# Attention with normalised queries and keys: one score tile moved, shared places for the third shift, a ring of 50, a one-product query scaling

## The chip, the cores and the metric

One core of a Trainium2 chip runs the whole kernel in one launch. The metric is the device time of an execution in microseconds; lower is better. The profile times one execution: its span runs from the first to the last instruction.

The engines are called PE (TensorE, with PEld for its weight loads), DVE (VectorE), ACT (ScalarE), POOL (GpSimd) and SP (SyncE, which here only issues DMAs). Each runs its own queue in order; semaphores tie them together.

## The reference

32 heads, 2048 positions, head size 20, everything in bfloat16. Queries and keys are brought to length one, the scores are scaled by one number per head, and softmax attention follows:

```
qn = q / (sqrt((q * q).sum(-1)) + eps)
kn = k / (sqrt((k * k).sum(-1)) + eps)
logits = einsum('bhqd,bhkd->bhqk', qn, kn) * t[None, :, None, None]
out = einsum('bhqk,bhkd->bhqd', softmax(logits), v)
```

So there are 32 x 2048 x 2048 scores, each of which needs an exponential, a product over 20 elements before it and one over 2048 positions behind it.

## The kernel before

**Units, waves, groups.** The scores of a head are cut into 64 units of 128 keys by 512 queries; four units (one for each group of 512 queries) make a tile, 16 tiles a head. Tiles go two ways. `DVE_TILES` (line 780) says how many of a head's tiles go to DVE: 5 to 7, 203 in all. The other 1236 units go to ACT.

**ACT's way.** Units are taken in waves of 2 and 3 in turn (`WAVES`), each with a slot of its own in `psA`. PE makes the scores (L1148 with 32 rows, or L1155 with 64 rows through the zero-padded `qz`), ACT takes the exponential of a whole wave in one instruction (L1254) and writes it to `p_ring`, a ring of `NP = 40` units. PE multiplies four units with `vaug`, V with a column of ones, into `psF` (L1176). An exponential may overwrite a place of the ring once the product that read it is done: `war` in `add_wave` (L1251) names that product.

**DVE's way.** A tile's scores come from `qP` (L1160), a scaled copy of the queries, as two matrix products into `psF`. The queries and keys carry three extra columns, which add the constants. DVE reads the 1024 sums per partition once (L1305), with one multiply and one add, as 32-bit integers into `xt`: each word holds two 16-bit floats, a bf16 and an fp16, which are approximate exponentials of two scores, so the 2048 scores of a partition's two query groups lie in 1024 words. Three more versions, each shifted by a constant of `PHASES`, are made by integer additions into `ss[0]`, `ss[1]` and `ss[2]`; the four versions are multiplied with V, scaled by `vph` (L959) for each shift, and so averaged (L1176, four sets of four matrix products of 512 columns).

A shift can be made in several ways: on POOL as an addition of 64-bit integers (L1335), in pieces or joined with the same shift of the next tile; on DVE as one addition (L1325), for two tiles at once (L1330), or, for the third shift alone, in a gapped form (L1323) that writes rows of 16 words at a pitch of 17 into a buffer of its own, `sp`. `xt` has `NX = 7` places, `ss[j]` and `sp` have `NE = 4`. `last_use` lists who last used a place; the third shift's list covers the plain and the gapped form together, so both buffers advance together.

**Preparation of a head.** Loads of q, k, v (L838); squares, sums and a reciprocal square root on DVE (L996 to L1024); the normalised rows to `qkn` (L1042); a transposing DMA to `qkT`; DMAs that copy keys in rotated order to `kR` and queries to `qz`. `qP` is made by DVE from `qkT` (L1052) as `qkT * pcol[:, 0] + pcol[:, 1]`, a scale and an addend per partition. Head 0 goes a faster way at the start: PE transposes, POOL copies the keys in three rotated orders (`rotk0`, L1128), and SP transposes these with three DMAs (L1130) to `kR`. The fills of constants stand ahead of that on DVE and POOL (L872 to L909); `kx` and the f32 queries of head 0 lie for that time in the last six units of `p_ring`.

**What sets the order.** A planner in the program (`Program.list_schedule`) simulates the engines with durations written at each `add` and fixes each queue's order before launch. Each task has a priority, mostly its due time in heads. Twenty-seven settings steer its choices, such as how long PE waits for a coming score product, or how many products of the last head may be left when the output bank is handed on (`FLIP`, `FSOON`). `STAGES` gives one number for each 10 us of planned time, which picks a value for each setting. `plan_waits` then writes the semaphore waits. Operations of DVE that the planner calls heavy, all but the reads, transposes and gapped shifts, are kept apart from POOL's additions.

The end of each head: DVE transposes the output (L1192), divides by the sums (L1201, L1209), SP stores.

Of the kernel before, what the change touches and what calls it, by code (L numbers as in the profile page):

```python
# [10 lines left out]
BF16 = mybir.dt.bfloat16  # L11
# [35 lines left out]
PAD = 16  # L47
# [34 lines left out]
class Program:  # L82
# [26 lines left out]
        "EASE": (0.0, 0.15, 0.3), "TWO": (1, 0), "HTR": (0.15, 0.0, 0.3, 0.5), "CONT": (1, 0), "HB": (1.2, 0.5, 0.8, 1.8, 2.4), "HLATE": (1.5, 0.5, 3.0),  # L109
        "WAITH": (0.3, 0.1, 0.6), "BLOG": (5, 3, 4, 7, 9, 99), "PTWO": (1, 0), "STAY": (1, 0), "URGE": (3, 2, 4, 6), "BOOST": (1.0, 0.0, 0.4, 4.0), "DPV": (0.0, 0.3, 0.65, 1.0), "FLIP": (0, 2, 4), "FSOON": (0.3, 0.0, 0.8), "JOIN": (0.8, 0.0, 0.4, 1.4), "MERGE": (0.0, 0.2, 0.4)}  # L110
    STAGES = (5971968, 5971971, 23941566379011, 52142628583944, 59302454818874, 69347322273448, 69347310327784, 70172875370728, 70172839538920, 69760057110760, 69699858183784, 80456615377947, 81282177248715, 81288065602227, 60796380404643, 60796380404648, 60803367607208, 60803367607208, 60829167996776, 68259239759720, 36985831402607, 71631643783891, 71633220411085, 71633220245185, 70033688337794, 70033690079630, 83314320437263, 27171772496628, 49440268483813, 34580101090789, 34580101090789, 34605895514005, 34605919401877, 34599469427608, 15611119408984, 15611107465048, 16436672321368, 16230281107289, 16230281107289, 37177604416007, 37177604416007, 6311176060947, 6311176060947, 13741312038101, 28601477959013, 75896859232048, 75896847288256, 68466969587152, 68466969587152, 75877676995213, 75829302561268, 75880900364788, 73400623713478, 73400086236358, 73400086237510, 83123322387687, 83123322387687, 83123322387687, 83123322387687, 82710539959527)

# [633 lines left out]
def bass_standalone__qk_norm__prompt_kernel(  # L746
# [12 lines left out]
    GORD = (0, 2, 1, 3)  # L759
    NP = 40  # L760
    NB = 8
    NV = 6
    NN = 4
    NT = 3
    NX = 7
    NE = 4
# [12 lines left out]
    DLM = 2  # L779
    DVE_TILES = [5, 6, 6, 6, 7, 6, 7, 6, 7, 6, 7, 6, 7, 6, 7, 6, 6, 7, 6, 7, 6, 7, 6, 7, 6, 7, 6, 7, 6, 7, 6, 5]  # L780
    NDMAX = 8
# [8 lines left out]
    with ExitStack() as es:  # L790
# [11 lines left out]
        vph = sbuf("vph", [128, NV, len(PHASES), NDMAX, 32], FP16)  # L802
        pcol = sbuf("pcol", [128, 2], F32)
        sqs = sbuf("sq", [128, NSQ * 2 * R, D], BF16)
# [87 lines left out]
        zc = [add("POOL", "z", lambda e, tk: e.memset(pcol[:, 0:1], 1.0), 0.06, [], -98.9)]  # L892
        for g, val in ((3, HI_SCALE), (2, 1.0), (1, HI_SCALE)):
            zc.append(add("POOL", "z", lambda e, tk, g=g, val=val: e.affine_select(
                pcol[:, 0:1], pcol[:, 0:1], [[1, 1]], ALU.is_ge, val, base=-32 * g, channel_multiplier=1),
                0.12, [zc[-1]], -98.8 + 0.01 * (3 - g)))
        zc.append(add("POOL", "z", lambda e, tk: e.memset(pcol[:, 1:2], 0.0), 0.06, [zc[-1]], -98.6))
        for p0, val in [(32 * g + D + i, x) for g in range(NG) for i, x in enumerate(
                (LO_REST,) if g % 2 else (HI_REST + HI_SHIFT * HI_SCALE, ROUND, -ROUND))]:
            zc.append(add("POOL", "z", lambda e, tk, p0=p0, val=val: e.affine_select(  # L900
                pcol[:, 1:2], pcol[:, 1:2], [[1, 1]], ALU.not_equal, val, base=-p0, channel_multiplier=1),
                0.12, [zc[-1]], -98.5 + 0.001 * p0))
        z_qz = [memset("POOL", qz[i][:, :, :], 0.0, 0.8, -81.5 + 0.1 * i) for i in range(NZ)]
        z_xt = [memset("POOL", xt[0][:, :].rearrange("p (n w) -> p n w", w=TILE)[:, :, 2048:TILE], 0.0, 0.2, -82)]
# [146 lines left out]
        def add_qp(h, deps):  # L1051
            qp[h] = add("DVE", f"qp{h}", lambda e, tk: e.tensor_scalar(  # L1052
                qP[h % NT][:, :], qkT[h % NT][:, 0:512], pcol[:, 0:1], pcol[:, 1:2], ALU.mult, ALU.add),
                0.323, deps + zc[-1:] + ([lambda: qk_users[h - NT]] if h >= NT else []), h - QLEAD if h else -26.1)
# [32 lines left out]
        def first_head(rinv):  # L1087
# [38 lines left out]
            for dl in range(1, 4):  # L1126
                for (g0, s0, m) in ((0, dl, 4 - dl), (4 - dl, 0, dl)):
                    cp.append(add("POOL", "rotk0", lambda e, tk, dl=dl, g0=g0, s0=s0, m=m: e.tensor_copy(  # L1128
                        kv[:, dl, :, g0:g0 + m, :], kv[:, 0, :, s0:s0 + m, :]), 0.2 + 0.11 * m, [nk], -90 + dl))
            rot[0] = [add("SP", "trnr0", lambda e, tk, dl=dl: e.dma_start_transpose(  # L1130
                kR[0][:, dl - 1, :].rearrange("p (c n) -> p c n", n=128), kx[:, 512 * dl:512 * dl + 512]), 1.3,
# [150 lines left out]
        def add_dgroup(jg):  # L1282
            j, = D_groups[jg]
            h, c, dl = D_tiles[j]
            ox, oe = place(0, NX, 1), place(1, NE, 1)
            bx, be = TILE * ox, TILE * oe
            old = lambda n, o: last_use.get((n, o), [])
# [4 lines left out]
            for bs in ((0,), (1,)) if SPLIT[j % len(SPLIT)] else ((0, 1),):  # L1292
# [17 lines left out]
                if TWICE[j % len(TWICE)]:  # L1310
                    reads.append(read(f"t1b.{j}.{bs[0]}", ss[2][0], be, W_ADD + PHASE_W[2], [qk] + old("s2", oe), due - 4.99))
                    again.append(reads[1])
# [3 lines left out]
            for i in range(len(PHASES)):  # L1316
                dst = ss[i][0]
                if i == 2 and again:
                    sh.append(again)
                    continue  # L1320
                def f_s(e, tk, i=i, dst=dst):
# [6 lines left out]
                def f_two(e, tk, i=i, dst=dst):  # L1328
                    a, b = (x[:, o:o + 2 * TILE].bitcast(I32).rearrange("p (n w) -> p n w", n=2)[:, :, 0:1024] for x, o in ((dst, be), (xt[0], bx)))
                    return e.tensor_scalar(a, b, float(PHASE_W[i]), None, ALU.add)  # L1330
# [3 lines left out]
                if jg >= 2:  # L1334
                    f.alt = lambda c, n, i=i, dst=dst: lambda e, tk: e.int64_add(  # L1335
                        dst[:, be + 2 * c:be + 2 * (c + n)].bitcast(I64), xt[0][:, bx + 2 * c:bx + 2 * (c + n)].bitcast(I64),
                        PHASE_W[i] * 0x100000001)
# [6 lines left out]
            def half(tile, o, g, f):  # L1344
                if f and f[0].slow:
                    return sp[:, oe, 512 // PAD * (g // 2):512 // PAD * (g // 2 + 1), :].bitcast(
                        FP16 if g % 2 else BF16).rearrange("p r (n w) -> p r n w", w=2)[:, :, 0:PAD, 1 - g % 2]
# [6 lines left out]
            for i, (tile, o, dep) in enumerate([(xt[0], bx, t1s)] + [(ss[n][0], be, sh[n]) for n in range(len(PHASES))]):  # L1354
                src = [] if i == 0 else dep
# [83 lines left out]
```

## Time and profile before

| | us |
|---|---|
| median of three runs | 579.21 (579.07 to 581.45) |
| the profiled execution | 579.11 |
| its span | 577.4 |
| ACT: busy / exponentials L1254, union of 495 | 563.0 / 559.5 |
| ACT: first exponential starts, last one ends | 8.03, 570.11 |
| DVE: busy; reads L1305, 203 x 1.217 | 556.7; 247.0 |
| DVE: gapped third shifts L1323, 159 x 1.222 | 194.0 |
| POOL: busy; additions L1335, 403 x 1.116 | 454.3; 442.4 |
| PE: busy | 551.6 |
| granted clock of PE | 1.0 |

In a row of the profile's groups stand the line, engine and operation, then what is written and read with shapes, the count, the busy time in us and the mean length of one in ns, and behind the second bar the idle time of the engine just before and what ended it. In the timeline a row can hold several instructions of one kind (x4): start, length of the whole row, engine, line. Where instructions of one engine overlap, busy time is their union, and the mean length is more than the distance between two of them.

### The profile page before, as it was taken

The numbers are of one execution on the slowest core, as the hardware profiler recorded it, in microseconds if no ns is written. First come the engines' busy times: TensorE is split into PE (matmuls) and PEld (weight loads), VectorE is DVE, ScalarE is ACT, GpSimd is POOL, SyncE is SP. The second block draws the span as 40 slices with busy tenths as digits, with TensorE's granted clock in tenths as the row PEclk, the third lists the DMA queues.
The fourth block names the chain that finished last, engine by engine and source line by source line (L and its number), as shares of the span: only waits on it lengthen the run. The fifth ranks groups of instructions, "written<-read, shape, count | busy, mean of one in ns | idle before, by whom it ended". The sixth has DMA issues, their size and how long they took to land.

```text
span 577.4 us, 14861 instructions
## 1 busy us (share of the span) xinstructions
PE 551.6 (96%) x6209; PEld 152.0 (26%) x6209; DVE 556.7 (96%) x662; ACT 563.0 (98%) x502; POOL 454.3 (79%) x455
## 2 busy tenths in 40 slices
PE   7898999999999999999999999999999999999997
PEld 2222222222222222222222222222222222222322
DVE  7999989999999999999999999999999999999996
ACT  6999999999999999999999999999999999999994
POOL 8377969779588858977688958887789877799974
PEclk9999999999999999999999999999999999999999
DMA  5553454522645444344244343343333333222000
GB/s 68 69 72 67 65 56 101 53 38 73 84 78 79 82 68 76 44 70 84 48 80 70 55 68 57 74 64 48 70 62 64 65 56 58 56 54 58 13 2 18
DMA packets 195763, 35.60 MB, mean 62 GB/s; under 512 B 172272, under 2 KB 195696, under 8 KB 195696
## 3 DMA queue, kind: packets, MB, share of 16 engines
q1 hardware_dynamic: 195552, 34.57, 37.1%
q8 instruction: 49, 0.80, 0.6%
q14 instruction: 18, 0.15, 0.1%
q10 hardware_dynamic: 144, 0.08, 0.1%
HBM read 7.87 MB, written 2.62 MB: 18 GB/s over the span
## 4 chain that ended last, share of the span: by engine, by line
ACT 94%; PE 3%; DVE 2%; issue 0%; DVEq 0%
ACT p_ring L1254 94%; PE psF L1176 2%; PE psF L1075 1%; DVE xt L1305 0%; PE psA L1148 0%; DVE ss L1325 0%; PE psF L1160 0%; PE psA L1155 0%; DVE oT L1192 0%; DVE rs_sum L999 0%; DVE qP L1052 0%; DVE ones L841 0%; DVE o_stage L1209 0%; DVE qkT L1122 0%; DVE qkT L1121 0%
## 5 line engine op out<-in xcount | busy, mean ns | idle before, releaser
L1254 ACT ACTIVATE p_ring<-psA 128x1024 bf16<-128x1024 f32 x495 | 559.5, 1464 | 3.2 <-PE psA L1148 2.2
L1335 POOL INT64_ADD ss<-xt x403 | 442.4, 1116 | 116.8 <-DVE qkn L1042 30.0
L1305 DVE TENSOR_SCALAR xt<-psF 128x1024 int32<-128x1024 f32 x203 | 247.0, 1217 | 7.9 <-PE psF L1160 6.9
L1323 DVE TENSOR_SCALAR sp<-xt 128x1040 int32<-128x1040 int32 x159 | 194.0, 1222 | 1.3 <-PE psF L1176 0.9
L1176 PE MATMUL psF<-ss,vph 128*32 128x512 f16 (+1 forms) x1800 | 163.0, 394 | 1.4 <-DVE vph L959 1.2
L1176 PE MATMUL psF<-p_ring,vaug 128*32 128x512 bf16 x1236 | 113.6, 383 | 0.0
L1148 PE MATMUL psA<-qkT,kR 32*128 32x512 bf16 x662 | 100.4, 385 | 7.8 <-ACT p_ring L1254 5.8
L1176 PE MATMUL psF<-xt,vaug 128*32 128x512 f16 (+1 forms) x812 | 81.4, 394 | 0.0
L1155 PE MATMUL psA<-qz,kR 64*128 64x512 bf16 x318 | 66.6, 386 | 3.3 <-ACT p_ring L1254 3.1
L1176 PE MATMUL psF<-sp,vph 128*32 128x512 bf16 (+1 forms) x636 | 66.7, 409 | 0.0
L1176 PEld LDWEIGHTS psF<-ss,vph 128*32 128x32 f16 x1800 | 41.6, 94 | 64.8 <-issue 40.9
L1160 PE MATMUL psF<-qP,kR 64*128 64x512 bf16 x278 | 53.6, 383 | 1.6 <-DVE xt L1305 1.3
L1148 PEld LDWEIGHTS psA<-qkT,kR 32*128 32x128 bf16 x662 | 24.6, 91 | 101.2 <-ACT p_ring L1254 98.7
L1176 PEld LDWEIGHTS psF<-p_ring,vaug 128*32 128x32 bf16 x1236 | 30.3, 94 | 41.0 <-issue 30.5
L1148 PE MATMUL psA<-qkT 32*128 32x512 bf16 x176 | 33.6, 384 | 3.8 <-ACT p_ring L1254 3.3
L1155 PEld LDWEIGHTS psA<-qz,kR 64*128 64x128 bf16 x318 | 16.3, 92 | 66.9 <-ACT p_ring L1254 65.6
L1176 PEld LDWEIGHTS psF<-xt,vaug 128*32 128x32 bf16 x812 | 21.0, 94 | 27.0 <-issue 22.2
L1192 DVE STREAM_TRANSPOSE oT<-psF 128x512 f32<-128x512 f32 x32 | 22.8, 711 | 5.0 <-PE psF L1176 4.7
L1160 PE MATMUL psF<-qP,qkT 64*128 64x512 bf16 x128 | 24.7, 382 | 1.1 <-DVE qP L1052 0.8
L1176 PEld LDWEIGHTS psF<-sp,vph 128*32 128x32 f16 x636 | 16.6, 94 | 26.2 <-issue 19.5
L1042 DVE TENSOR_TENSOR qkn<-qk_sb,rs_r 128x1280 bf16<-128x1280 bf16 (+1 forms) x17 | 23.3, 1383 | 0.0
L999 DVE TENSOR_REDUCE rs_sum<-sq 128x64 f32<-128x1280 bf16 (+1 forms) x17 | 23.0, 1352 | 0.0
(72 smaller groups left out, 178.6 us busy)
## 6 DMA issues: line engine op xcount, KB each, us to landing
kR<-qkT SPq DMA_DIRECT2D x62, 96.0 KB, 2.2
kR<-qkT SPq DMA_DIRECT2D x62, 64.0 KB, 2.1
qz<-qkT SPq DMA_DIRECT2D x104, 32.0 KB, 1.9
qk_sb<-in_k_dram SPq DMA_DIRECT2D x32, 80.0 KB, 3.0
vaug<-in_v_dram SPq DMA_DIRECT2D x32, 80.0 KB, 3.2
qk_sb<-in_q_dram SPq DMA_DIRECT2D x124, 20.0 KB, 2.5
out_dram<-o_stage SPq DMA_DIRECT2D x31, 80.0 KB, 1.7
kR<-qkT SPq DMA_DIRECT2D x62, 32.0 KB, 1.9
```

What stands on the lines that cost most here:

```text
L999: sums.append(dv("sum", lambda e, tk, i=i, m2=m2, src=src: e.tensor_reduce(rs["sum"][:, 2 * R * i:2 * R * i + m2], src, AXIS_X, ALU.add), ...
L1042: norm[h] = [dv("norm", lambda e, tk, x=x, b=b, i=i, m=m: e.tensor_tensor(qkn_all[:, b:b + m, :, :].rearrange("p n r w -> p (n r) w")[:, : ...
L1075: warm.append(add("PE", "warm", lambda e, tk: e.matmul(psO[0], ones[:, 0:128], ones[:, :], start=True, stop=True), PE_MM, [z_one], -300))
L1148: return eng.matmul(dst, k_of(h, c, (rho - g) % 4, ps), qkT[h % NT][ps, 0:512], tile_position=(32 * g, 0))
L1155: return eng.matmul(dst, k_of(h, c, (rho - g) % 4, ps), qz[h % NZ][ps, g % 2, :], tile_position=(64 * b, 0))
L1160: return eng.matmul(dst, k_of(h, c, dl, ps), qP[h % NT][ps, :], tile_position=(64 * b, 0))
L1176: last = eng.matmul(psO[h % 2][32 * g:32 * g + 32, :], w_of(g), rhs_of(g), start=start, stop=False, skip_group_check=True, tile_position=( ...
L1192: trO[h] = add("DVE", f"tr{h}", lambda e, tk: e.transpose(oT_all[:, so, :, :].rearrange("p r d -> p (r d)"), psO[h % 2]), 0.63, [lambda: p ...
L1254: act[w] = add("ACT", f"exp{w}", lambda e, tk: e.activation(p_ring[:, p0 * 512:p0 * 512 + n], psA[:, slot * WAVES[0] * 512:slot * WAVES[0] ...
L1305: return add("DVE", name, lambda e, tk: e.tensor_scalar(dst[:, o + 2 * w0:o + 2 * (w0 + n)].bitcast(I32), psF[:, prog.pair_of[j] + w0:prog ...
L1323: return e.tensor_scalar(sp[:, oe, :, :].bitcast(I32)[:, :, 0:PAD], xt[0][:, bx:bx + TILE].bitcast(I32), float(PHASE_W[i]), None, ALU.add)
L1335: f.alt = lambda c, n, i=i, dst=dst: lambda e, tk: e.int64_add(dst[:, be + 2 * c:be + 2 * (c + n)].bitcast(I64), xt[0][:, bx + 2 * c:bx + ...
```

## The change

- `DVE_TILES` has 202 tiles in all instead of 203: the larger counts are spread a little differently, and one tile goes to ACT.
- `sp` is gone. The third shift's gapped form is written to the same place of `ss[2]` as its plain form; a place of `ss[2]` is 2212 elements of 16 bits long (the gapped form needs 2210), where the others keep 2080. The third shift is no longer joined with the next tile's.
- The ring `p_ring` has 50 units instead of 40, `xt` 8 places instead of 7.
- `qP` is `qkT * pcol`, one product, with a bf16 scale per partition. The addends move into the three extra columns of the queries and keys, which are filled with other constants (two fills more for each `qkn` tile, one more for `kx`), and `pcol` needs 12 selects for its places instead of 8.
- The fills of `qz` on POOL wait for the rotated copies of head 0.
- `FLIP` and `FSOON` have one more choice each, and `STAGES` holds 57 new numbers instead of 60.

```
-"FLIP": (0, 2, 4), "FSOON": (0.3, 0.0, 0.8)
+"FLIP": (0, 2, 4, 8), "FSOON": (0.3, 0.0, 0.8, 3.0)
...
-    NP = 40
+    NP = 50
...
-    NX = 7
+    NX = 8
...
-    DVE_TILES = [5, 6, 6, 6, 7, 6, 7, 6, 7, 6, 7, 6, 7, 6, 7, 6, 6, 7, 6, 7, 6, 7, 6, 7, 6, 7, 6, 7, 6, 7, 6, 5]
+    DVE_TILES = [5, 6, 6, 6, 7, 6, 7, 6, 7, 6, 6, 7, 6, 7, 6, 7, 6, 6, 7, 6, 7, 6, 6, 7, 6, 7, 6, 7, 6, 7, 6, 5]
...
-        pcol = sbuf("pcol", [128, 2], F32)
+        pcol = sbuf("pcol", [128, 1], BF16)
...
-        ss = [[sbuf(f"ss{j}", [128, NE * TILE], I16)] for j in range(len(PHASES))]
-        sp = sbuf("sp", [128, NE, ROWS, 2 * PITCH], I16)
+        SIZES = [TILE, TILE, max(TILE, (ROWS * 2 * PITCH + 3) // 4 * 4)]
+        ss = [[sbuf(f"ss{j}", [128, NE * SIZES[j]], I16)] for j in range(len(PHASES))]
+
+        def gapped(o):
+            return ss[2][0][:, o:o + ROWS * 2 * PITCH].rearrange("p (r w) -> p r w", w=2 * PITCH)
...
-        z_kx = add("DVE", "z", lambda e, tk: e.memset(kxp[:, 0:R, D:D + 3], 1.0), 0.15, [z_kx0], -96.9)
+        z_kx = add("DVE", "z", lambda e, tk: e.memset(kxp[:, 0:R, D:D + 2], 1.0), 0.15, [z_kx0], -96.9)
+        z_kx = add("DVE", "z", lambda e, tk: e.memset(kxp[:, 0:R, D + 2:D + 3], -1.0), 0.12, [z_kx], -96.8)
...
-                qkn[i][:, R:2 * R, D:D + 3], 1.0), 0.12, [z], -94.9 + i))
+                qkn[i][:, :, D + 1:D + 3], 1.0), 0.12, [z], -94.95 + i))
+            z_qkn[-1] = add(eng, "z", lambda e, tk, i=i: e.memset(
+                qkn[i][:, R:2 * R, D:D + 1], 1.0), 0.1, [z_qkn[-1]], -94.9 + i)
+            z_qkn[-1] = add(eng, "z", lambda e, tk, i=i: e.memset(
+                qkn[i][:, R:2 * R, D + 2:D + 3], -1.0), 0.1, [z_qkn[-1]], -94.85 + i)
...
-                (LO_REST,) if g % 2 else (HI_REST + HI_SHIFT * HI_SCALE, ROUND, -ROUND))]:
+                (0.0, LO_REST, 0.0) if g % 2 else (-HI_REST / HI_SHIFT, ROUND, ROUND))]:
...
-        z_qz = [memset("POOL", qz[i][:, :, :], 0.0, 0.8, -81.5 + 0.1 * i) for i in range(NZ)]
+        rotk0 = []
+        z_qz = [add("POOL", "z", lambda e, tk, i=i: e.memset(qz[i][:, :, :], 0.0), 0.95, [lambda: rotk0], -81.5 + 0.1 * i) for i in range(NZ)]
...
-                qP[h % NT][:, :], qkT[h % NT][:, 0:512], pcol[:, 0:1], pcol[:, 1:2], ALU.mult, ALU.add),
+                qP[h % NT][:, :], qkT[h % NT][:, 0:512], pcol[:, 0:1], None, ALU.mult),
...
-            bx, be = TILE * ox, TILE * oe
+            bx, es_ = TILE * ox, [z * oe for z in SIZES]
...
-                            sp[:, oe, :, :].bitcast(I32)[:, :, 0:PAD], xt[0][:, bx:bx + TILE].bitcast(I32), float(PHASE_W[i]), None, ALU.add)
+                            gapped(be).bitcast(I32)[:, :, 0:PAD], xt[0][:, bx:bx + TILE].bitcast(I32), float(PHASE_W[i]), None, ALU.add)
...
-                    if chained.get(i) and ox and oe:
+                    if i < 2 and chained.get(i) and ox and oe:
```

More of the change, by code (lines that the diff above doesn't have):

```diff
@@ L888, in bass_standalone__qk_norm__prompt_kernel @@
             z_qkn.append(add(eng, "z", lambda e, tk, i=i: e.memset(
-                qkn[i][:, R:2 * R, D:D + 3], 1.0), 0.12, [z], -94.9 + i))
+                qkn[i][:, :, D + 1:D + 3], 1.0), 0.12, [z], -94.95 + i))
[3 more added lines that the diff above has]
+                qkn[i][:, R:2 * R, D + 2:D + 3], -1.0), 0.1, [z_qkn[-1]], -94.85 + i)
             z_qkn[-1] = add(eng, "z", lambda e, tk, i=i: e.memset(
                 qkn[i][:, 0:R:2, D:D + 1], -float(HI_SHIFT)), 0.1, [z_qkn[-1]], -94.8 + i)
-        zc = [add("POOL", "z", lambda e, tk: e.memset(pcol[:, 0:1], 1.0), 0.06, [], -98.9)]
+        zc = [add("POOL", "z", lambda e, tk: e.memset(pcol[:, :], 1.0), 0.06, [], -98.9)]
         for g, val in ((3, HI_SCALE), (2, 1.0), (1, HI_SCALE)):
             zc.append(add("POOL", "z", lambda e, tk, g=g, val=val: e.affine_select(
-                pcol[:, 0:1], pcol[:, 0:1], [[1, 1]], ALU.is_ge, val, base=-32 * g, channel_multiplier=1),
+                pcol[:, :], pcol[:, :], [[1, 1]], ALU.is_ge, val, base=-32 * g, channel_multiplier=1),
                 0.12, [zc[-1]], -98.8 + 0.01 * (3 - g)))
-        zc.append(add("POOL", "z", lambda e, tk: e.memset(pcol[:, 1:2], 0.0), 0.06, [zc[-1]], -98.6))
         for p0, val in [(32 * g + D + i, x) for g in range(NG) for i, x in enumerate(
-                (LO_REST,) if g % 2 else (HI_REST + HI_SHIFT * HI_SCALE, ROUND, -ROUND))]:
+                (0.0, LO_REST, 0.0) if g % 2 else (-HI_REST / HI_SHIFT, ROUND, ROUND))]:
             zc.append(add("POOL", "z", lambda e, tk, p0=p0, val=val: e.affine_select(
-                pcol[:, 1:2], pcol[:, 1:2], [[1, 1]], ALU.not_equal, val, base=-p0, channel_multiplier=1),
+                pcol[:, :], pcol[:, :], [[1, 1]], ALU.not_equal, val, base=-p0, channel_multiplier=1),
                 0.12, [zc[-1]], -98.5 + 0.001 * p0))
-        z_qz = [memset("POOL", qz[i][:, :, :], 0.0, 0.8, -81.5 + 0.1 * i) for i in range(NZ)]
+        rotk0 = []
+        z_qz = [add("POOL", "z", lambda e, tk, i=i: e.memset(qz[i][:, :, :], 0.0), 0.95, [lambda: rotk0], -81.5 + 0.1 * i) for i in range(NZ)]
         z_xt = [memset("POOL", xt[0][:, :].rearrange("p (n w) -> p n w", w=TILE)[:, :, 2048:TILE], 0.0, 0.2, -82)]
@@ L1129, in first_head @@
                         kv[:, dl, :, g0:g0 + m, :], kv[:, 0, :, s0:s0 + m, :]), 0.2 + 0.11 * m, [nk], -90 + dl))
+            rotk0.extend(cp)
             rot[0] = [add("SP", "trnr0", lambda e, tk, dl=dl: e.dma_start_transpose(
@@ L1310, in add_dgroup @@
                 if TWICE[j % len(TWICE)]:
-                    reads.append(read(f"t1b.{j}.{bs[0]}", ss[2][0], be, W_ADD + PHASE_W[2], [qk] + old("s2", oe), due - 4.99))
+                    reads.append(read(f"t1b.{j}.{bs[0]}", ss[2][0], es_[2], W_ADD + PHASE_W[2], [qk] + old("s2", oe), due - 4.99))
                     again.append(reads[1])
@@ L1345, in half @@
                 if f and f[0].slow:
-                    return sp[:, oe, 512 // PAD * (g // 2):512 // PAD * (g // 2 + 1), :].bitcast(
+                    return gapped(o)[:, 512 // PAD * (g // 2):512 // PAD * (g // 2 + 1), :].bitcast(
                         FP16 if g % 2 else BF16).rearrange("p r (n w) -> p r n w", w=2)[:, :, 0:PAD, 1 - g % 2]
@@ L1353, in weight @@
                 return vph[:, h % NV, i - 1, r - (R - nd_v(h)), :] if i else vaug[h % NV][:, r, :]
-            for i, (tile, o, dep) in enumerate([(xt[0], bx, t1s)] + [(ss[n][0], be, sh[n]) for n in range(len(PHASES))]):
+            for i, (tile, o, dep) in enumerate([(xt[0], bx, t1s)] + [(ss[n][0], es_[n], sh[n]) for n in range(len(PHASES))]):
                 src = [] if i == 0 else dep
```

11 lines of the change are left out of this document (6 added, 5 removed).

## The prediction

> **What bounds the kernel now.** I read the page's busy shares first, then the chain of work that ended last, then ScalarE's waits and its timeline from exponential to exponential, and last the first 18 us and the last 10 us of the timeline.
>
> ```profile
> span 577.4 us, 14861 instructions
> PE 551.6 (96%) x6209; PEld 152.0 (26%) x6209; DVE 556.7 (96%) x662; ACT 563.0 (98%) x502; POOL 454.3 (79%) x455
> ACT 94%; PE 3%; DVE 2%; issue 0%; DVEq 0%
> ...
> L1254 ACT ACTIVATE p_ring<-psA 128x1024 bf16<-128x1024 f32 x495 | 559.5, 1464 | 3.2 <-PE psA L1148 2.2
> ```
>
> Three engines are above 95%, but the chain that ended last is ScalarE's exponentials (L1254) for 94% of the span. They lose only 3.2 us to recorded idle time. The timeline of ScalarE alone shows where:
>
> ```profile
> 8.03 3.28 ACT L1254 ACTIVATE p_ring<-psA 128x1024 bf16<-128x1024 f32 x3 [0.57 <-PE psA L1148]
> 12.07 2.37 ACT L1254 ACTIVATE p_ring<-psA 128x1536 bf16<-128x1536 f32 x2 [0.75 <-PE psA L1148]
> 15.34 429.96 ACT L1254 ACTIVATE p_ring<-psA 128x1536 bf16<-128x1536 f32 x380 [0.91 <-PE psA L1148]
> 446.13 123.98 ACT L1254 ACTIVATE p_ring<-psA 128x1536 bf16<-128x1536 f32 x110 [0.83 <-PE psF L1176]
> ```
>
> The first column is the start, the second the length, in brackets the idle time before. Exponentials run from 8.03 to 570.11 with three stops: two in the first 16 us (waiting for scores), one at 445 us. That one waits for PE's L1176, the product with V, which must free places of the ring of 40. Successive records overlap (a record of 3 units lasts 1.68 us, yet the next starts 1.33 to 1.35 us after it; 2 units: 0.90 to 0.92). Taking the start of every exponential, 19 gaps exceed 0.895 (2 units) or 1.33 (3 units) by over 0.08 us, 5.9 us in all: 0.90 and 1.03 at the start, 1.25 at 444 us (the ring), 2.75 in sixteen others. Those 5.9 us are all that a better order can give while the exponentials last.
>
> The end is another matter:
>
> ```profile
> 573.36 0.41 PE L1176 MATMUL psF<-p_ring,vaug 128*32 128x512 bf16 x4
> 573.82 0.72 DVE L1192 STREAM_TRANSPOSE oT<-psF 128x512 f32<-128x512 f32 x1 [2.64 <-PE psF L1176]
> 574.57 0.25 DVE L1201 RECIPROCAL rec<-oT 128x16 f32<-128x16 f32 x1
> 574.85 0.49 DVE L1209 TENSOR_TENSOR o_stage<-oT,rec 128x320 bf16<-128x320 f32 x1
> 575.37 0.33 SPq L838 DMA_DIRECT2D out_dram<-o_stage  x1
> ```
>
> ScalarE is done at 570.11, but PE works on until 573.79: from 568.64 it does nothing but products with V, 22 sets of four in 5.15 us, 0.234 us a set. So 3.68 us of the end are PE's backlog; VectorE waits 2.64 us for it. From 573.79 to the end of the span are 3.61 us that nothing in the change touches. The profiled execution took 579.11 us, 1.71 more than its span; the median of the runs shown is 579.21, 0.1 above it.
>
> **The change, part by part.**
>
> *202 tiles in place of 203.* One tile (2x1024 scores) moves from VectorE to ScalarE: four units more, 1240 in place of 1236. The waves become 248 pairs of 2 and 3 units, where 247 pairs and a last single stood. A pair costs 0.905 + 1.34 = 2.245 us from start to start, and the single is the last row's 0.85 us, of which some 0.43 us is its own half of the 0.90 of two units: **+1.8 us**, on the path, hidden by nothing. VectorE loses one read (1.217 us, L1305) and, as 159 of 203 tiles have their third shift there (1.222 us, L1323), on average 0.96 us: -2.2 us. POOL loses two shifts of about 1.04 us. PE loses 1 + 4 sets and gains 1.6 + 1: -2.4 x 0.234 = -0.56 us, less 0.05 for switches between kinds. PE's part counts where PE sets the end: **-0.5 us** in the tail. VectorE and POOL (20.7 and 123 us not busy) don't set the end, so I count theirs at nothing directly.
>
> *Ring of 50.* A wave waits for the product that read its place 50 units earlier in place of 40, 10 x 0.452 = 4.5 us more leeway (559.5 us over 1236 units). The one ring wait of the trace goes: **-1.25 us**. What is late next is PE itself: a bigger ring does not make it faster, and up to 10 more units (2.5 sets, 0.6 us) can wait at the end. Bounds: -1.25 to +0.6; I take -1.25, as the tail's backlog is counted above.
>
> *Shared places of the third shift.* Plain and gapped form of one tile now lie in one buffer. Before, both were already guarded by one list of last users per place, so no new wait arises; the shapes stay the same (1040 words, 1.222 us). The third shift is no longer joined with that of the next tile on POOL. At most 44 third shifts are not in the gapped row; a joined job saves a fixed part that the rows do not show alone, bounded by 0 and 1.04 us, a whole job. It lies in POOL's idle time (116.8 us before L1335), so nothing; uncovered, PE's next product would wait. Eight places of xt in place of seven: VectorE's waits before a read are for scores (6.9 us <- L1160), not for places, so nothing.
>
> *Query scaling as one product.* Thirty-two instructions on VectorE with one bf16 scalar in place of two f32 ones:
>
> ```profile
> L1052 DVE TENSOR_SCALAR qP<-qkT,pcol 128x512 bf16<-128x512 bf16 x32 | 13.2, 420 | 0.0
> L959 DVE TENSOR_SCALAR vph<-vaug 128x352 f16<-128x352 bf16 x42 | 9.4, 245 | 0.0
> L959 DVE TENSOR_SCALAR vph<-vaug 128x176 f16<-128x176 bf16 x12 | 2.1, 197 | 0.0
> ```
>
> The two rows of L959, with constants as scalars, grow by 48 ns for 176 elements, 0.27 ns each; at that slope 512 elements last 197 + 336 x 0.27 = 288 ns. So the new form costs between 0.29 and 0.42 us, and VectorE gains 0 to 32 x 0.13 = 4.2 us. I take 0.35, halfway, as neither row has its kind of scalar. It lies on VectorE, off the path: nothing directly. A rule speaks against a gain: the Trainium skill ("DVE: scalar operands, raw-bit mode, write accounting and state across instructions", 1. Scalar operands) says that a bf16 scale costs the same as an fp32 one; by it this term is 0 and the sum is as it is. No row here has a bf16 scalar.
>
> *Constants and fills at the start.* On POOL pcol needs 12 selects of 0.19 us where it needed 8, and one fill (0.10) less; the three tiles of qkn on POOL get two more fills each (0.13 to 0.17 us): +1.6 us. A fill of qz (0.97 us, at 5.62) leaves the stretch before the six rotating copies: net +0.5 us ahead of copies that began at 6.75, just after their input (6.69). Two fills of qz now stand ahead of vph's (1.32 us, ended 11.31), whose first reader runs at 12.90: cover 1.6 us for a shift of 0.97. VectorE gets three small fills more (0.07 to 0.10 each, up to 0.19 apart) in the 0.62 us that it idles before 3.10: hidden. The copies feed three transposing DMAs on SP's queue (issued from 7.95, 2.5 us to landing), for which the wave at 12.07 waits: bounds -0.06 (the copies start with their input) to +0.5; the second stop (15.34) is PE standing 1.5 us behind the scaled V and can vanish (-1.0) with another order. I take 0 for the start.
>
> *A new order of everything.* The planner's settings are all replaced and its choices widened, so who waits for whom changes in each stretch. The sixteen small stops (2.75 us) come from late operands; with 2.2 to 6.4 us less on VectorE I let a quarter go: **-0.7 us**. Bounds: -2.75, and upward rival 2.
>
> Sum: 579.11 + 1.8 - 0.5 - 1.25 - 0.7 = **578.5 us**, 0.6 below its own time, 0.7 below the median.
>
> **The rivals.**
>
> 1. *The backlog at the end goes (faster).* PE's relief and a better order leave it nearly empty when the last exponential ends: the tail falls from 3.68 to about 1.2 us (the last group's set, 0.4, a handover, two or three sets), 2.0 beyond the 0.5 counted; with the small stops gone for the most part (1.3 more): 578.5 - 2.0 - 1.3 = 575.2. For it: PE had idle time in every stretch of 100 us from 20 to 520 (2.2 to 5.1 us), yet ended late, which is a matter of order. Against: from 520 to 570.2 PE was busy 49.7 of 50.2 us, and a deeper ring invites a backlog. Chance 0.25.
>
> 2. *PE stands behind late operands (slower than before).* PE's queue is in order; a product with V placed before its shift is done holds the next scores, and ScalarE stops. Price from the rows: 0.9 us of ScalarE for one (at 14.10, where PE waited 1.52) to 1.25 (the longest stop, at 444, of another cause); I take 1.15. Places: where third shifts fall to POOL, or where products were put off by the deeper ring. To pass the bound it takes four such blocks: 578.5 + 4 x 1.15 = 583.1. For it: all three engines are above 95%. Against: the order of before had one such block in 550 us. Chance 0.17.
>
> 3. *The change does not do what it says.* The ring's extra places stay unused because products wait for something else, and the small stops stay: 578.5 + 1.25 + 0.7 = 580.45. Chance 0.10.
>
> **How the numbers follow.** About 0.5% (2.9 us) is what a measurement of this kernel can tell from no change: 576.3 to 582.1. The forecast has chance 0.48, its own range 576.5 to 581. It and rival 3 lie within: same 0.58; rival 1 gives faster 0.25, rival 2 slower 0.17. The range of 8 in 10 reaches to both outer cases, 574.9 to 583.2; the unknown costs (start -1.1 to +0.5, ring +1.85, small stops -2.05, tail -2.0) span the same.
>
> **What would show it.** Right: 496 exponentials, the last ending near 570.7; no ScalarE wait for L1176; 202 reads; a tail of about 3.2 us from the last exponential to PE's last product; L1052 between 290 and 420 ns. Wrong: a tail under 2 us (rival 1), several ScalarE stops of about 1 us after 20 us (rival 2), a first stop that grows with the copies, or a pair slower than 2.245 us, since 0.01 us on each of 248 pairs is 2.5 us.

## The result and the profile after

The changed kernel takes 582.23 us, the median of 20 runs (580.93 to 584.33), beside 579.9 for the kernel before in the same runs (20, 579.07 to 584.44): a ratio of 1.0036 with the interval 1.0022 to 1.005. It is slower by 0.36%; 578.5 was forecast. The profiled executions show the same: spans of 577.4 us before and 580.1 after, 2.7 apart.

The page of the changed kernel, in the rows shown of before: the span, busy time by engine, the chain that ended last by engine, and the group of exponentials, now on line 1264.

```profile
span 580.1 us, 14874 instructions
PE 552.1 (95%) x6191; PEld 151.2 (26%) x6191; DVE 554.5 (96%) x666; ACT 564.4 (97%) x503; POOL 451.1 (78%) x452
ACT 90%; PE 7%; DVE 2%; issue 1%
...
L1264 ACT ACTIVATE p_ring<-psA 128x1024 bf16<-128x1024 f32 x496 | 560.9, 1508 | 5.6 <-PE psA L1158 5.6
```

There are 496 exponentials, as forecast. Their recorded idle time rose from 3.2 to 5.6 us, and none of it is for L1186, the product with V (L1176 before). ACT's timeline (start, length of the row, idle time before it in brackets) shows where the idle time went:

```profile
8.00 3.28 ACT L1264 ACTIVATE p_ring<-psA 128x1024 bf16<-128x1024 f32 x3 [0.57 <-PE psA L1158]
11.83 3.71 ACT L1264 ACTIVATE p_ring<-psA 128x1536 bf16<-128x1536 f32 x3 [0.55 <-PE psA L1158]
18.94 1.02 ACT L1264 ACTIVATE p_ring<-psA 128x1024 bf16<-128x1024 f32 x1 [3.40 <-PE psA L1158]
21.02 552.89 ACT L1264 ACTIVATE p_ring<-psA 128x1536 bf16<-128x1536 f32 x489 [1.06 <-PE psA L1158]
```

From 21.02 on, 489 exponentials run without a recorded stop, to 573.91: the stop at 445 us is gone. But ahead of 18.94 ACT stands idle for 3.40 us, which it never did before. DVE's last transpose, behind PE's last product, starts at 576.54 in place of 573.82, 2.72 us later. I take the loss apart by ACT's gaps from the start of one exponential to the start of the next, counted as in the prediction (stops: gaps of over 0.08 us beyond 0.895 and 1.33):

| | before | after | difference | forecast |
|---|---|---|---|---|
| first exponential starts | 8.03 | 8.00 | -0.03 | 0 |
| four units more: a wave of 0.905 and a last one of 1.74 in place of 0.85 | | | +1.80 | +1.8 |
| stops up to 20 us | 2.14 | 5.40 | +3.26 | 0 |
| stops from 20 us on, the one at 444 us included | 3.79 | 1.49 | -2.30 | -1.95 |
| remainder: the ordinary gaps, 248 pairs | | | +1.07 | 0 |
| last exponential ends | 570.11 | 573.91 | +3.80 | -0.15 by the terms (570.7 was written) |
| from there to PE's last product | 3.68 | 2.58 | -1.10 | -0.5 |
| from there to the end of the span | 3.61 | 3.61 | 0 | 0 |

Two of these rows, the stops behind 20 us and the remainder, are partly made by counting starts. A record starts before the one ahead of it ends, and the overlap can shrink and grow. In the kernel before, around the gap of 0.30 us too much at 298.30, and further on:

```profile
297.11 1.27 ACT L1254 ACTIVATE p_ring<-psA 128x1024 bf16<-128x1024 f32 x1
298.30 1.45 ACT L1254 ACTIVATE p_ring<-psA 128x1536 bf16<-128x1536 f32 x1
299.64 1.02 ACT L1254 ACTIVATE p_ring<-psA 128x1024 bf16<-128x1024 f32 x1
...
344.53 1.34 ACT L1254 ACTIVATE p_ring<-psA 128x1024 bf16<-128x1024 f32 x1
345.44 1.77 ACT L1254 ACTIVATE p_ring<-psA 128x1536 bf16<-128x1536 f32 x1
```

The start at 298.30 is 0.30 us late, but the end, 299.75, comes 1.37 us behind the last one, where 1.34 is usual: 0.03 us are lost. Behind it the records are short and grow again from wave to wave, to 1.34 and 1.77 us; while they grow, starts come 2.234 us a pair apart and ends 2.260. Counted by ends, a pair takes 2.260 us (0.917 and 1.343) in both kernels wherever ACT does not stop, and the 3.80 us come out without a remainder: -0.04 for the first exponential's end, +1.77 for four units more, +3.24 for the stops up to 22 us (2.08 before, 5.32 after), -1.17 for those behind (1.17 before, 0.94 of it at 446.13, and none after).

One row is wrong in kind, the start. Here are DVE and POOL in its first stretch, after the change:

```profile
9.46 1.84 POOL L912 MEMSET qz<- 128x1024 bf16 x2
10.07 3.41 DVE L1337 TENSOR_SCALAR ss<-xt 128x1024 int32<-128x1024 int32 x1
...
11.30 1.32 POOL L845 MEMSET vph<- 128x1440 f16 x1
...
12.80 0.14 POOL L845 MEMSET nil<- 128x32 bf16 x1
...
13.80 0.68 DVE L1337 TENSOR_SCALAR ss<-xt 128x1024 int32<-128x1024 int32 x1
...
15.93 1.21 DVE L1315 TENSOR_SCALAR xt<-psF 128x1024 int32<-128x1024 f32 x1
```

The same instruction, the plain shift of one tile (L1337), takes 0.68 us at 13.80 and 3.41 at 10.07. POOL fills without a pause from 9.21 to 12.94, and the long shift ends at 13.48, 0.68 after POOL began its last small fill at 12.80. The two fills of `qz`, both of which now stand behind the rotated copies, are 1.84 us of that. Before, the same place looked so:

```profile
9.99 1.32 POOL L841 MEMSET vph<- 128x1440 f16 x1
10.31 2.28 DVE L1325 TENSOR_SCALAR ss<-xt 128x1024 int32<-128x1024 int32 x2
11.25 1.44 POOL L841 MEMSET vaug<- 128x176 bf16 x2
```

Two shifts in 2.28 us, where 1.3 is normal: the first (1.55 us) already waited for the end of the `vph` fill, and then POOL's small fills waited (1.44 us for what takes 0.35 elsewhere). The sign was there to be read.

From DVE the delay travels to PE and ACT. The next read of scores (L1315) starts at 15.93, where it started at 14.66 before. PE's next product for DVE needs that read's bank, and PE's scores for ACT stand behind it in the queue:

```profile
17.20 0.61 PE L1170 MATMUL psF<-qP,kR 64*128 64x512 bf16 x2 [3.47 <-DVE xt L1315]
18.29 0.60 PE L1158 MATMUL psA<-qkT,kR 32*128 32x512 bf16 x2
```

Then a second loss follows. PE's busy time and granted clock by stretches of 4 us (length, busy time, clock, DMA share, GB/s):

```profile
12.00:16.00 4.00, 1.04 (x9) 1.00 0.70 62
16.00:20.00 4.00, 2.80 (x20) 0.63 0.70 56
20.00:24.00 4.00, 4.00 (x46) 0.94 0.37 70
```

While PE waited it was busy for 1.04 of 4 us, and then its clock fell to a mean of 0.63: products last 0.60 and 0.61 us where 0.39 is usual, and ACT waits a further 1.06 us ahead of 21.02.

### The profile page after: what moved, and what is told of

Read it like the earlier page. It is cut to its first block, busy times and chain, and to the rows that moved or that the text cites. A ratio compares the mean times of both kernels' runs of the same rounds, so it can differ in the third digit from the quotient of the medians.

```text
span 580.1 us, 14874 instructions
## 1 busy us (share of the span) xinstructions
PE 552.1 (95%) x6191; PEld 151.2 (26%) x6191; DVE 554.5 (96%) x666; ACT 564.4 (97%) x503; POOL 451.1 (78%) x452
## 4 chain that ended last, share of the span: by engine, by line
ACT 90%; PE 7%; DVE 2%; issue 1%
ACT p_ring L1264 90%; PE psF L1186 4%; PE psF L1084 1%; PE psA L1158 1%; PE psF L1170 1%; PE psA L1165 1%; DVE xt L1315 1%; DVE rs_sum L1008 0%; DVE oT L1202 0%; DVE ss L1337 0%; PE psF L1091 0%; DVE ones L845 0%; DVE o_stage L1219 0%; DVE sq L1005 0%; DVE qkT L1131 0%
## 5 line engine op out<-in xcount | busy, mean ns | idle before, releaser
L1315 DVE TENSOR_SCALAR xt<-psF 128x1024 int32<-128x1024 f32 x202 | 245.8, 1217 | 10.9 <-PE psF L1170 9.7
L1186 PE MATMUL psF<-ss,vph 128*32 128x512 bf16 x2424 | 217.2, 399 | 0.2 <-DVE xt L1315 0.2
L1335 DVE TENSOR_SCALAR ss<-xt 128x1040 int32<-128x1040 int32 x158 | 192.8, 1223 | 0.9 <-PE psF L1186 0.8
L1186 PE MATMUL psF<-p_ring,vaug 128*32 128x512 bf16 x1240 | 112.5, 383 | 0.0
L1186 PE MATMUL psF<-xt,vaug 128*32 128x512 bf16 (+1 forms) x808 | 81.5, 395 | 0.1
L1186 PEld LDWEIGHTS psF<-ss,vph 128*32 128x32 f16 x2424 | 53.8, 94 | 93.5 <-issue 67.6
L1186 PEld LDWEIGHTS psF<-p_ring,vaug 128*32 128x32 bf16 x1240 | 30.2, 94 | 41.3 <-issue 30.4
L1186 PEld LDWEIGHTS psF<-xt,vaug 128*32 128x32 bf16 x808 | 21.0, 95 | 27.3 <-issue 20.9
L1165 PE MATMUL psA<-qz,qkT 64*128 64x512 bf16 x80 | 20.2, 387 | 0.5 <-ACT p_ring L1264 0.3
L1170 PEld LDWEIGHTS psF<-qP,kR 64*128 64x128 bf16 x276 | 13.5, 94 | 25.8 <-issue 16.0
```

Source lines behind the costliest of these rows:

```text
L1165: return eng.matmul(dst, k_of(h, c, (rho - g) % 4, ps), qz[h % NZ][ps, g % 2, :], tile_position=(64 * b, 0))
L1170: return eng.matmul(dst, k_of(h, c, dl, ps), qP[h % NT][ps, :], tile_position=(64 * b, 0))
L1186: last = eng.matmul(psO[h % 2][32 * g:32 * g + 32, :], w_of(g), rhs_of(g), start=start, stop=False, skip_group_check=True, tile_position=( ...
L1315: return add("DVE", name, lambda e, tk: e.tensor_scalar(dst[:, o + 2 * w0:o + 2 * (w0 + n)].bitcast(I32), psF[:, prog.pair_of[j] + w0:prog ...
L1335: return e.tensor_scalar(gapped(be).bitcast(I32)[:, :, 0:PAD], xt[0][:, bx:bx + TILE].bitcast(I32), float(PHASE_W[i]), None, ALU.add)
```

## The experiments

**Two theories.** Theory 1: a plain shift of DVE and a fill of POOL exclude each other, so fills beside the first shift are what makes the kernel slower. Theory 2: the new order of work, or the data that it makes late, does it, and fills beside DVE only look guilty. In all kernels below the order of every other instruction is kept as the program had planned it; only what is named is moved.

**a: the two fills of `qz` beside DVE's second and third read of scores.**

```
+        park(z_qz[0], "t1.1.0", 0.95)
+        park(z_qz[1], "t1.2.0", 0.95)
```

`park` lets a fill start when the instruction ahead of the named one on DVE is done, here so that it runs while DVE reads.

> The changed kernel with one thing moved: POOL's two fills of qz start beside VectorE's second and third read of scores (which read PSUM) and no longer beside its first shift. Everything else keeps its place in every queue. Theory 1 (a fill on POOL and a packed shift of VectorE cannot run at once): the first shift, 3.41 us in the changed kernel, waits only for the vph fill and falls to about 1.5 us; ScalarE's stop of 3.4 us falls to about 1 or 1.5; the time falls by 2.0 to 2.7 us, ratio to before about 1.000. Theory 2 (the shift is late because of the new order of VectorE's and PE's queues, and the fills only lie beside it): first shift and stop stay, time within 0.3 us of the changed kernel.

Measured: 579.7 (578.45 to 583.86), ratio 1.0002 (0.9983 to 1.0021). The first shift:

```profile
9.54 1.33 POOL L845 MEMSET vph<- 128x1440 f16 x1
10.10 1.64 DVE L1337 TENSOR_SCALAR ss<-xt 128x1024 int32<-128x1024 int32 x1
```

3.41 has become 1.64: what is left is the wait for the `vph` fill, which ends at 10.87, and for two small fills behind it. The loss against before is gone. (The profiled execution is the longest of the twelve, 583.86, with PE's clock at 0.50 from 16 to 28 us, so its stops behind that are not compared.)

**b: the kernel before, with its first fill of `qz` put behind the six copies**, as the change does, and nothing else.

```
+        p = prog.order["POOL"]
+        i = p.index(z_qz[0])
...
+        f = p.pop(i)
+        i = p.index(z_qz[1])
+        p.insert(i, f)
```

> The kernel before with one thing moved: POOL's first fill of qz stands behind the six rotating copies, so that both fills are followed by the vph fill, as in the changed kernel; no other queue is touched. Theory 1: the first shift of VectorE, which starts at 10.31, waits 0.95 us longer, and ScalarE's second stop grows by 0.9 to 2 us; time up by 1 to 2 us, ratio 1.002 to 1.0035. Theory 2: the time stays within 0.3 us of before.

Measured: 580.66 (579.84 to 582.23) beside 580.25, ratio 1.0016 (1.0003 to 1.003): slower, with the tiles, the ring and otherwise the order of before.

```profile
8.89 1.83 POOL L841 MEMSET qz<- 128x1024 bf16 x2
10.10 1.91 DVE L1325 TENSOR_SCALAR ss<-xt 128x1024 int32<-128x1024 int32 x2
...
11.45 1.86 POOL L841 MEMSET vph<- 128x1440 f16 x1
13.35 0.40 DVE L959 TENSOR_SCALAR vph<-vaug 128x176 f16<-128x176 bf16 x2 [0.95 <-POOL vph L841]
```

The first shift did not wait 0.95 us longer, as was expected: here the shifts got in after the `qz` fills (0.6 us late), and it was then POOL that waited: the small fills stretched to 1.44, `vph`'s came late, and DVE stood 0.95 us for it. The second stop of ACT grew from 1.03 to 1.96; PE's clock fell here too, to a mean of 0.67 from 16 to 20 us, where it stayed at 1.00 before, and what that adds was not separated. So the cost depends on who comes first: the moved fill costs about 0.9 us with this order (580.25 x 0.0016) and 3.3 of stops with that of the change. Why the shifts got in between the fills here and not there was not settled.

**c: the changed kernel with longer fills**: ahead of each `qz` fill one of 512 elements into a place that nobody reads.

```
+            (e.memset(dose[:, 512 * i:512 * i + 512], 0.0), e.memset(qz[i][:, :, :], 0.0))[1]
```

> The changed kernel with each of the two qz fills preceded by a fill of 512 elements of a buffer that nothing reads (about 0.5 us each, 1.0 us in all). Theory 1: the first shift's record grows from 3.41 to about 4.4 us and ScalarE's long stop by about 1.0 us: 583.2. Theory 2: VectorE's shift keeps its length, the time stays at 582.2.

Measured: 583.3 (581.2 to 585.35), ratio 1.0062 (1.0041 to 1.0083), against 1.0036 for the change.

```profile
9.55 0.52 POOL L913 MEMSET dose<- 128x512 bf16 x1
10.02 0.95 POOL L913 MEMSET qz<- 128x1024 bf16 x1
...
10.15 4.36 DVE L1338 TENSOR_SCALAR ss<-xt 128x1024 int32<-128x1024 int32 x1
```

Each added fill takes 0.47 us to the start of the next, 0.94 for both, and the shift lasts 0.95 us longer (4.36 against 3.41); ACT's stop grew from 3.53 to 4.47. In the trace the dose passes through one to one; by the times alone the step (1.0062 against 1.0036) is not clear, as the two intervals overlap.

**d: no long fill beside the first shift.** The `qz` fills are parked, and `vph`'s is cut in two: 240 columns, which head 0 needs, at once, and the other 1200 beside a read.

```
+        z_vph.fn = lambda e, tk: e.memset(vph[:, 0:1, :, :, D + 2:32], 0.0)
+        z_rest = Task("POOL", "z", lambda e, tk: e.memset(vph[:, 1:NV, :, :, D + 2:32], 0.0), 1.1, [], 0.0)
...
+        park(z_rest, "t1.1.0", 1.1)
+        park(z_qz[0], "t1.2.0", 0.95)
+        park(z_qz[1], "sum1", 0.95)
...
+        p.insert(p.index(z_rest), z_qz[1])
```

> As the run with the moved fills, and the vph fill is cut in two: the part that head 0 needs (240 of 1440 elements) stays, the rest stands beside VectorE's second read; the two qz fills stand beside the sum of squares of head 1 and the third read. Theory 1: the first shift takes its plain 0.7 us, the long stop falls below 1 us; 0.6 to 1.2 us less than the run with moved fills alone, about 578.5. Theory 2: no change from the changed kernel.

Measured: 579.16 (577.82 to 579.43), ratio 0.998 (0.9968 to 0.9992): faster than both kernels.

```profile
10.27 0.69 DVE L1337 TENSOR_SCALAR ss<-xt 128x1024 int32<-128x1024 int32 x1
12.03 0.95 POOL L912 MEMSET qz<- 128x1024 bf16 x1 [2.01 <-DVE ss L1337]
12.62 0.91 DVE L1337 TENSOR_SCALAR ss<-xt 128x1024 int32<-128x1024 int32 x1
```

The first shift is back at 0.69. The one at 12.62 still loses 0.23 to the tail of a fill. The first three stops are 0.69, 0.37 and 0.47 in place of 0.69, 3.53 and 1.18; the span is 576.4. Theory 2 has fallen: only fills were moved, the order of all other work stayed, and 3.7 us of span went with them.

**e: the ring alone.** The kernel before, with 50 units in the ring and the order of before (to make room, the third shift's two forms share their places as in the change).

```
-    NP = 40
+    NP, NR = 40, 50
...
-        p_ring = sbuf("p_ring", [128, NP * 512], BF16)
+        p_ring = sbuf("p_ring", [128, NR * 512], BF16)
...
+                if u >= NR:
+                    act[w].deps.append(pv_of_group[(u - NR) // 4])
```

> The kernel before with nothing changed but the ring: 50 units instead of 40 (the third shift and its gapped form share their places, to make room), every queue in the order of before. Theory: the one stop that ACT makes for the ring (1.25 us at 444 us) goes and nothing takes its place: -1.25, a ratio of 0.998; ACT's pairs keep the pace of before, 2.247 us, if the pace belongs to the order of the work. Rival A: the stop was also held by late operands of PE's products and stays or moves: -0.3 to 0. Rival B: the slower pace of after (2.258 us a pair, +1.1 in all) belongs to the larger ring and its addresses: the gain is eaten, 0 within 0.3.

Measured: 579.42 (579.01 to 581.49) beside 579.73, ratio 0.999 (0.9973 to 1.0006). The theory, like the prediction, said that the stop at 444 us would go. It moved:

```profile
448.25 121.72 ACT L1257 ACTIVATE p_ring<-psA 128x1536 bf16<-128x1536 f32 x108 [0.66 <-PE psA L1151]
```

Before, ACT waited ahead of 446.13 for L1176 (a place of the ring), and the gap was 1.25 us too long. With ten places more ACT runs on for two waves and then waits ahead of 448.25 for L1151, its next scores, with a gap 1.10 too long. PE's queue is the same in both kernels, and it is laid around that stop: the planner's list has it too, its exponentials 384 and 385 starting 1.99 us apart where 0.90 is usual, and puts eight sets of products between the scores that PE makes at 445.38 and those at 447.81, where two to four stand between those just ahead. So the larger ring alone takes away 0.15 of the 1.25 us (by ends 0.17 of 0.94); what the order did for the ring stays. From 75 to 125 us a pair takes 2.260 us by ends here, before and in the change, so there is no slower pace that the ring could have made: it was one of starts only. Rival A holds, with the order in place of late operands; rival B falls.

**g: the start of d in the kernel before.**

```
+        park(z_rest, "t1.1.0", 1.1)
+        park(z_qz[1], "t1.2.0", 0.95)
```

with `vph`'s fill cut as in d.

> The kernel before with the start of d: vph's fill cut in 240 and 1200 columns, the larger part and the second fill of qz beside DVE reads. Theory: the start stops 0.90 + 1.03 + 0.21 = 2.14 us fall to 1.0 to 1.3, so -0.8 to -1.1, a ratio of 0.9985, which says that the start of before was already hurt by POOL's fills. Rival: the stop at 13.41 us is set by PE's or DVE's own work and not by fills: 0 within 0.3.

Measured: 578.05 (577.44 to 580.76), ratio 0.9967 (0.9951 to 0.9983). The two first shifts take 1.30 us in place of 2.28, and ACT's stops up to 20 us are 0.79 and 0.21: 1.0 in place of 2.14.

```profile
10.17 1.30 DVE L1325 TENSOR_SCALAR ss<-xt 128x1024 int32<-128x1024 int32 x2
```

The kernel before was hurt by the same collision, in a smaller size: it cost its second stop. The span is 576.4, that of d, and the intervals of the two ratios overlap, so no difference between the two kernels is shown once both have a clean start. It is not shown that there is none: d's median is 1.1 us above g's. Where PE's mean clock was 0.999 or more, the times are alike (577.8 to 578.2 for d, 577.4 to 578.7 for g), but that was so in five of d's twelve executions and in eleven of g's.

**i: e and g together.**

> e and g together: the kernel before, its order of the steady part, its 203 tiles and its two-scalar product, with a ring of 50 and a start free of fills. If the two add up: -1.25 - 0.95 = -2.2, about 577.8 beside 580.0, below d (after with a clean start, -0.8 to -1.1), by the slower pace and the unit more of after. Rival: what the clean start gives is lost again by the ring or at the end: no better than g.

Measured: 577.79 (577.27 to 580.13), ratio 0.9968 (0.9951 to 0.9986). It is the lowest median of the study, but not to be told from g, so it is not shown that the two gains add up. The profiled execution has a stop of 1.56 us ahead of 214.72; just before it DVE's squares (L999) wait 2.02 us for the load of the next queries, and the next read follows late:

```profile
211.60 0.82 DVE L999 TENSOR_TENSOR sq<-qk_sb 128x1280 bf16<-128x1280 bf16 x1 [2.02 <-DMA qk_sb<-in_q_dram]
```

In g and e the stops near there are 0.48 and 0.23. But this execution took 579.02 us, and seven of the other eleven took 577.27 to 577.91, so they can hardly have had that stop. Whether the time gained at the start brought it about is open.

**f: d with the small fills of `vaug` and `xt` behind the first two copies.**

```
+        i = p.index(rotk0[1]) + 1
+        for u in late:
+            p.insert(i, u)
```

> d with the small fills of vaug and xt put behind POOL's first two copies of the rotated keys, so that these copies, which the transposes by DMA wait for, start earlier. Theory: the first stop (0.69 us at 10.25) shortens by 0.2 to 0.4 and the rest is that of d: a ratio of 0.9975 against 0.998 for d. Rival: the small fills then lie beside DVE's first shift and hold it, as the large ones did: 0.3 to 1.0 longer than d.

Measured: 579.79 (578.39 to 580.89), ratio 0.9975 (0.9954 to 0.9996), not to be told from d. The first copy starts at 6.77 (6.82 in d): its input is ready at 6.43, but POOL is at four selects of `pcol` from 5.43 to 6.84. The fills end later, the first shift takes 0.97 in place of 0.69, and the first three stops are 0.84, 0.64 and 0.44. The theory was wrong, and the rival right as far as the trace shows: 0.4 us more of stops.

**j: d with two scalars in the query product.**

```
-                qP[h % NT][:, :], qkT[h % NT][:, 0:512], pcol[:, 0:1], None, ALU.mult),
+                qP[h % NT][:, :], qkT[h % NT][:, 0:512], pcol[:, 0:1], zcol[:, 0:1], ALU.mult, ALU.add),
```

> d with one part of the change undone: the query product takes a second scalar again (a column of zeros is added), in all 33 products. Theory: the products go back from 0.37 to about 0.42 us each (1.6 us of DVE in all), DVE has that much idle or spare before each of ACT's units, and the time stays that of d: within 0.3 of it, the same stops. Rival: DVE stands ahead of PE everywhere, so that some of the 1.6 us show up as stops of ACT: +0.5 to +1.6.

Measured: 579.22 (577.89 to 579.63), ratio 0.998 (0.9969 to 0.9992), the same as d. The product goes from a mean of 374 ns in d (median 346) to 435 (median 406), and the median of before, with two f32 scalars, was 406 too:

```profile
L1062 DVE TENSOR_SCALAR qP<-qkT,pcol,zcol 128x512 bf16<-128x512 bf16 x32 | 13.6, 435 | 0.1
```

So the 0.06 us of each product come from the second scalar and its addition, not from the number format. The Trainium skill ("DVE: scalar operands, raw-bit mode, write accounting and state across instructions", 1. Scalar operands) says that a bf16 scale costs what an fp32 one does, and the two medians of 406 agree. And some 2 us of DVE in all show no cost in time here.

**k: a pause of ACT in d**, two exponentials of 512 elements near 347 us.

```
+        for n in range(2):
+            f = Task("ACT", "pause", lambda e, tk, n=n: e.activation(dose[:, 512 * n:512 * n + 512], ones[:, :], ACT.Exp, scale=LN2), 0.5, [a[k - 1]], 0.0)
...
+            a.insert(k, f)
```

> d with a pause put into ACT's queue: two exponentials of 512 elements into a place that nobody reads, ahead of the first exponential after 340 us of the plan, inside a stretch where ACT's pairs take 2.260 us. It asks whether a stop resets ACT's pace. Theory P: after a stop ACT has the operands ready and runs at 2.234 us a pair for some 40 us, as the stretches behind the large stops of before do, so that a pause of about 1.0 us costs only 0.4 to 0.7. Theory Q: the pace belongs to the work of that stretch and not to stops: pairs of 2.260 on both sides, the cost is the whole pause, 0.9 to 1.1.

Measured: 580.22 (578.91 to 583.13), ratio 0.9999 (0.9984 to 1.0015), 1.06 above d by the medians. The gap at the pause is 1.06 us too long, and the pairs take 2.260 us from 300 to 346 us and from 351 to 396, as in d. (Its profiled execution is a long one, 583.13, with the clock at 0.50 from 16 to 24 us; the pause lies far behind that.) Theory P has fallen: the pause costs its whole length. It is work of ACT's own, so k does not show a wait; but behind the wait at 446.13 in the kernel before a pair takes 2.260 us by ends as well, from 447 to 500 us. The 2.234 us that Theory P went by are those of starts.

## Why the prediction was wrong

- **The start, taken as 0 between -1.1 and +0.5: this step failed.** It asked who reads what the fills write, found 1.6 us of cover for the `vph` fill, and called its delay of 0.97 us hidden. It did not ask what DVE does while POOL fills. a, c and d show that DVE's plain shift waits for the fills: +3.26 us of stops, more than the whole difference of the two spans (2.7); the last of them, 1.18, came after PE's clock had dropped. The row that said it, a pair of shifts at 10.31 taking 2.28 us, was in the trace of before.
- **A rule that was not weighed.** The Trainium skill ("SBUF — State Buffer", Who interferes with whom) says that DVE in its two-port modes and GpSimd share a pair of ports as an exclusive lock, and that the one that comes second waits for the other's whole instruction. The trace agrees and goes further: at 10.07 DVE waited not for one fill but for several in a row, 2.73 us beyond its 0.68. The ports themselves show in no run.
- **Four units more, +1.8:** +1.80 (by ends +1.77), right.
- **The ring, -1.25: the number nearly came out, the reason only in part.** In the change the stop at 444 us is gone, but by ends it had cost 0.94, and e shows that 50 places by themselves take away 0.15 of the 1.25: the order had to be made anew for the rest. The new order does use the ring: counted along PE's instructions, scores run up to 50 units ahead of their product, and up to 43 before. Whether it could have avoided the stop with 40 places is open.
- **Small stops, -0.7: mis-sized.** The prediction took gaps between starts for time lost ("5.9 us are all that a better order can give"). By ends the sixteen small ones of 2.75 us had cost some 0.4, of which 0.20 at 17.80, so 0.7 was not there to win. In the table they are 1.05 of the -2.30, and the ordinary gaps give them back (+1.07).
- **PE's tail, -0.5:** -1.10; twice the size, in the direction of rival 1, which put the tail at 1.2 us (measured 2.58).
- **The pace, "a pair slower than 2.245 us" among what would show it wrong:** by starts it came, +1.07 us in 248 pairs, but it means nothing: by ends a pair takes 2.260 us in both kernels, and the 2.245 was that of starts with an overlap that still grew.
- **The query product, 0.35 between 0.29 and 0.42:** a median of 346 ns and a mean of 372, right, off the path as said (j).
- **The rivals.** None had the mechanism. Rival 2 had the sign, PE behind late operands, but put it in the steady part, where the change has no stop of over 0.04 us by ends. Without its start the change is what was forecast, somewhat below before: +1.80 - 2.30 + 1.07 - 1.10 = -0.5 us; by luck in part, as the small stops and the ordinary gaps cancel. d and g have the same span, d with 1.5 us of stops at its start and g with 1.0.

What each part of the change would bring by itself, the 202 tiles above all, was not separated: the settings of the planner belong to one exact set of sizes, so a part taken alone comes with another order of everything.

## What to carry to other kernels

When work is moved to "a queue with room", ask what the neighbour engine executes in that stretch, not only who reads the result: the fills of POOL cost DVE's shift 2.73 us, a dose of 0.94 more cost 0.95 more, and ACT's stop grew by as much. The same instruction at two lengths in one trace (0.68 and 1.55 us) is a sign to follow before anything is put beside it. Where the order is fixed beforehand, a wait is woven into it: with a larger ring alone, the stop moved to the next thing that the order had placed for it. And where the records of an engine overlap, count from end to end before a late start is priced: one of 0.30 us cost 0.03 here.

## What the runs showed of the hardware

- DVE's shift, ready at 10.07, waited through six fills of POOL in a row (two of `qz`, a small one, `vph`, two of `vaug`). Its end less its plain 0.68 us is 12.80, where POOL's last small fill starts; in a, c, f and k the same reckoning gives 11.06, 13.83, 10.59 and 10.22, and the last small fill starts at 11.05, 13.82, 10.58 and 10.21. Before and in b the shifts got in between two fills.
- Fills and reads of PSUM go together: L1315 beside a fill of 0.95 or 1.10 us took 1.21 in d, as elsewhere.
- ACT's exponentials end 0.917 us (2 units) or 1.343 us (3 units) behind the one ahead, in every kernel here. Their records overlap by up to 0.42 us; a late start uses up the overlap first, and it comes back by 0.013 us a wave.
- PE's clock drops within the first 20 us when PE has waited, and not always for the same wait. Its mean was 0.999 or more in 14 of the 31 executions of before that stand beside a to d, in five of d's 12, in eleven of g's, and in none of the change's 20. Two executions with PE busy for the same 2.33 of 4 us, d and then j:

```profile
12.00:16.00 4.00, 2.33 (x22) 1.00 0.70 63
16.00:20.00 4.00, 4.00 (x52) 1.00 0.72 60
```

```profile
12.00:16.00 4.00, 2.33 (x22) 0.98 0.68 61
16.00:20.00 4.00, 4.00 (x39) 0.59 0.66 58
```

d's third stop is 0.47 us and j's 1.45, and d's and j's runs fall into two clusters some 1.1 us apart (577.8 to 578.3 and 579.1 to 579.6). The Trainium skill ("TensorE: Matmul & The Clock Gate", What's actually happening) says that the window in which activity is counted runs freely and does not start with the kernel, which fits two outcomes for one wait. The stretches at a clock of 0.50 last 3.41 us in the change (17.04 to 20.46) and 13.65, four times as long, in a (15.06 to 28.71), as they would with a window of one length. How busy a window must be to keep the clock no run here settles.
